# Two small GpSimd copies behind each scatter and gather of the experts

## The chip, the cores and the metric

The kernel runs on one NeuronCore of one Trainium2 chip. The metric is the device time of one execution in microseconds (us). Before the change it is 939.87 us, the median of 3 runs (939.29 to 940.05).

Engines are called as the profile calls them: PE is TensorE (matrix products, transposes), DVE is VectorE, ACT is ScalarE, POOL is GpSimd, SP is SyncE, which here only starts DMAs. "L941" is line 941 of the kernel before.

## The reference, cut to what matters

The first half is attention over 8 batches and 8 heads, 576 positions, head size 64: scores, a threshold at the row's maximum minus `tau`, softmax over what stays, times `v`. Its output is laid out as 4608 rows of 512 numbers. The second half is a mixture of 8 experts in which a row's expert follows from a hash of its token id:

```python
expert_idx = token_ids * np.int64(2654435761) % np.int64(E)
out = np.zeros((N, D), dtype=np.float32)
for e in range(E):
    mask = expert_idx == e
    xe = x[mask]
    h = np.maximum(xe @ w1[e], 0.0)
    out[mask] = h @ w2[e]
```

`w1` is 8 x 512 x 1024, `w2` is 8 x 1024 x 512, all in fp32. The change lies in the second half alone.

## The kernel before, in words

**Attention (to about 475 us).** The loop over 32 pairs of heads keeps PE, DVE and ACT in step. POOL does small work there: one threshold of 128x2 per tile (`thr`, L253), a scaling of the keys (`k_sb`, L215), and, between these, 36 indirect DMAs that write token numbers to slots in HBM (L542) and later 20 gathers for the first expert (L119). The slots come back as `stok` and `stok_odd`, 128 partitions x 8 experts x 19 int32, 152 numbers in each partition. L807 takes the smaller of the two into `stok`; after that nobody reads `stok_odd`. From `stok` come `gidx_x` (rows to gather) and `qidx` (where to scatter).

**Experts (from about 500 us).** The experts run in an order by size; the ones here are numbered in that order, 0 to 7. For expert e, layer 1 makes h = relu(w1 x) and layer 2 makes w2 h. Each layer is a two by two block product made with seven block products and sums of blocks (`seven`, L926). PE runs the seven products of a group one after the other (L941); layer 1 has two groups (g = 0, 1) of 7 x 8 matmuls, layer 2 one group of 7 x 16. PSUM has four tiles for them (`sc` and `bank`, two each), so a product may start when the product four before it has been read. DVE reads them (L861: `u`, `h`, `oT`), ACT copies the first of each group (L951, `p`) and applies the relu to finished blocks of h (L948). The sums of blocks of w1, w2, x and h that the next products need are DVE instructions too (L858 and some of L861), both of whose inputs lie in SBUF; the readers of products have one input in PSUM.

**Rows in.** `fetch(e)` (L1045) issues five gathers of 128 rows of 512 fp32 on POOL (L119) into the five `xg` buffers. DVE transposes each in 32x32 squares into `xq` (L1056), 16 DMAs of SP move `xq` into `xT` (L1064), and DVE makes the sums of x from it. `fetch(e + 2)` is called in layer 2 of expert e, at step 2; the transpositions of `xg` for expert e + 1 run in layer 1 of e and at the start of layer 2. For e = 1 a copy of one element (`mark`, L1049) stands ahead of every gather and waits for a block of h.

**Rows out.** `put_squares(e, i)` (L1024) transposes half of expert e's output into `o_q[i]` on DVE (L1028) and then issues 8 to 10 scatters of 128 pieces of 128 fp32 each on POOL (L1036). The first half is called in layer 2 of e at step 3, the second in layer 1 of e + 1. There are 17 scatters for expert 0, 18 for 1 to 4, 19 for 5 and 6. Expert 7 is put out in another way (`put_out`, four scatters, and `last_tile`, one). In program order, POOL's work is thus: the gathers of `fetch(e + 2)`, the scatters of expert e, the gathers of `fetch(e + 3)`, and so on. In the trace a run of scatters and the gathers behind it form one burst without breaks, and then POOL is idle until the next half of an output has been transposed.

**What sets the order.** The order of each engine is the one in which the code issues (`manual_schedule`); semaphores are placed by the framework. An indirect DMA of POOL takes the next of eight DMA semaphores, and waits until the DMA eight before it has landed. A gather also waits until DVE has transposed the buffer that it overwrites. A transposition into `o_q[i]` waits for the scatters that read `o_q[i]` last time. The scatters do not wait for one another's rows (`declare_no_dep`). The weights are loaded by SP two experts ahead.

Of the kernel before, what the change touches and what calls it, by code (L numbers as in the profile page):

```python
# [20 lines left out]
def kernel(  # L21
# [12 lines left out]
    nc = tc.nc  # L34
# [3 lines left out]
    E, _, F = w1.shape  # L38
# [60 lines left out]
    stok = consts.tile([P, E, NB], I32, name="stok")  # L99
    stok_odd = consts.tile([P, E, NB], I32, name="stok_odd")  # L100
# [17 lines left out]
    def gather(src, dst, idx):  # L118
        nc.gpsimd.indirect_dma_start(  # L119
            out=dst, out_offset=None, in_=src,  # L120
            in_offset=bass.IndirectOffsetOnAxis(ap=idx, axis=0),
            bounds_check=src.shape[0] - 1, oob_is_err=False)
# [704 lines left out]
    with tc.tile_pool(name="m_x", bufs=1) as m_x, \  # L827
# [169 lines left out]
        def put_out(e, *groups):  # L997
# [14 lines left out]
            for tr, kts in zip(trs, groups):  # L1012
                for i, kt in enumerate(kts):
# [7 lines left out]
                        nc.scalar.copy(dst, src)  # L1021
                    put_rows(o_sb[0:rows], gidx[0:rows, kt:kt + 1])

        def put_squares(e, i):  # L1024

            n_half = caps[e] // 64
            s0, s1 = ((0, n_half), (n_half, -(-caps[e] // 32)))[i]
            nc.vector.transpose(  # L1028
                out=o_q[i][:, 0:s1 - s0].rearrange("p n a c -> p c n a"),
                in_=oT[:, :, 32 * s0:32 * s1].rearrange("p c (n q) -> p c n q", q=32))  # L1030
            for s in range(s0, s1):
                put_rows(o_q[i][:, s - s0].rearrange("p a c -> p (a c)"), qidx[:, e, s:s + 1],
                         rows=out_q)

        def put_rows(o_sb, idx, ordered=False, rows=out):
            inst = nc.gpsimd.indirect_dma_start(  # L1036
                out=rows[:, :], out_offset=bass.IndirectOffsetOnAxis(ap=idx, axis=0),
                in_=o_sb, in_offset=None, bounds_check=rows.shape[0] - 1, oob_is_err=False)
            inst = getattr(inst, "ins", inst)
            if ordered:  # L1040
                return
            tc.declare_no_dep(inst, group="rows", reason="every token has one slot: distinct rows")
            tc.add_to_no_dep_group("rows", inst)

        def fetch(e):  # L1045
            for k in range(KT):
                if e == 1:

                    nc.gpsimd.tensor_copy(mark[0:1, :], h_0[0:1, k, 0:1])  # L1049
                gather(x_dram, xg_bufs[k][:], gidx_x[:, e, k:k + 1])  # L1050

        def turn_x(e):


            def squares(k):
                return lambda: nc.vector.transpose(  # L1056
                    out=xq[:, :, 32 * k:32 * k + 32],
                    in_=xg_bufs[k][:].rearrange("p (d a) -> p d a", a=32))

            def move():  # L1060
                for g in range(4):
                    s0, s1 = 32 * KT * g, min(32 * KT * (g + 1), caps[e])
                    for r in range(4):
                        nc.sync.dma_start(out=xT_bufs[e % 2][32 * r:32 * r + 32, :, s0:s1],  # L1064
                                          in_=xq[32 * g:32 * g + 32, r::4, 0:s1 - s0])

            return [squares(k) for k in range(KT)] + [move]

        with tc.manual_schedule():
            run(sums_w2(0), 4)  # L1070
            fill(18)
            late_h(lambda fo: (ps_sc.tile([P, 2, 512], FP32, name="sc") if fo in (2, 4) else
                               ps_m.tile([P, 2, 512], FP32, name="bank2")))
            fetch(1)
            run(sums_h(0, 0, FH), 4)

        with tc.manual_schedule():
            for e in range(E):
# [3 lines left out]
                if e > 0:  # L1082
                    w2_work, h_work = sums_w2(e), sums_h(e, 0, 2)

                    def side1(g, step):
                        if g == 0:
                            run(w2_work)
                            if step == 0:
                                put_squares(e - 1, 1)
                        else:  # L1090
                            run(h_work)
                        if step > 2:
                            run(turns, 1 if g == 0 else 2)

                    layer1(e, side1)
                    run(sums_h(e, 2, FH), 4)
                x_work = (sums_w1(e + 1) + sums_x(e + 1)) if more else []

                def side2(step):
                    if step == 0:  # L1100
                        run(turns, len(turns))
                    else:
                        run(x_work, 2)
                    if step == 2 and e + 2 < E:
                        fetch(e + 2)
                    if step == 4 and e + 2 < E:
                        load_w1(e + 2)
                    if more and step == 3:
                        put_squares(e, 0)
                    if not more and step == 4:  # L1110
                        put_out(e, (0,))
# [85 lines left out]
```

## Time and profile before

| | |
|---|---|
| time, median of 3 runs | 939.87 us |
| the profiled execution's own time | 931.3 us |
| its span, first to last instruction | 929.7 us |
| mean granted clock of TensorE | 0.996 |
| PE busy | 909.8 us, 98% |
| DVE busy | 757.5 us, 81% |
| ACT busy | 457.3 us, 49% |
| POOL busy | 403.7 us, 43% |
| scatters of experts 0 to 6 (L1036) | 127, mean 1.09 us |
| gathers for experts 1 to 7 (L119) | 35, mean 1.04 us |

One execution is profiled; all lines of the profile are from it. A group's line has the source line, the engine, the operation, what is written and read with its shape, how often, then the busy time in us with the mean of one in ns, and then the idle time of the engine just before these instructions with what ended it. A line of the timeline has start and duration in us, engine, source line, operation, and in brackets the idle time before it and who ended it; "issue" means that the profile shows nothing that was waited for, "remote" an unknown releaser. A busy time "by stretch" has the stretch, its length, the busy time of PE with the count of its instructions, the granted clock, the share of DMA time and GB/s. A line of waits has who waited for whom, and then us in total, how often, and the longest.

Ends of matmuls are modelled in the trace; their starts are recorded.

### The profile page before, as it was taken

How to read it: one execution, taken by the hardware profiler on the slowest of the kernel's cores; microseconds unless marked ns; L12 is line 12 of the kernel's file. 1: busy time of each engine (PE TensorE's matmuls, PEld its weight loads, DVE VectorE, ACT ScalarE, POOL GpSimd, SP SyncE). 2: the span in 40 equal slices, each digit the busy share in tenths (PEclk: the TensorE clock that was granted, in tenths of full speed). 3: DMA queues.
4: the chain of work that ended last, by engine and by line, in shares of the span. 5: the costliest groups of instructions: out<-in, count | busy, mean ns of one | idle time of the engine just before them, and what ended most of it. 6: DMA issues, size and time to landing. Idle time of an engine off the chain costs nothing.

```text
span 929.7 us, 20725 instructions
## 1 busy us (share of the span) xinstructions
PE 909.8 (98%) x7495; PEld 662.0 (71%) x7495; DVE 757.5 (81%) x1654; ACT 457.3 (49%) x741; POOL 403.7 (43%) x528
## 2 busy tenths in 40 slices
PE   7999999999999999999999999999999999999996
PEld 4666666656666566665678888788887978878785
DVE  7999999999999999999955776767668676777551
ACT  6888888888888898888812010110201021020110
POOL 4232432456666623455423370724527073440702
PEclk9999999999999999999999999999999999999999
DMA  7354463554545668743101745364372536412101
GB/s 175 92 148 118 109 152 93 136 131 103 123 105 153 159 165 214 216 107 88 30 25 51 237 131 158 133 173 141 95 223 75 164 133 165 157 34 50 48 3 55
DMA packets 114775, 113.11 MB, mean 122 GB/s; under 512 B 32475, under 2 KB 89315, under 8 KB 114672
## 3 DMA queue, kind: packets, MB, share of 16 engines
q1 hardware_dynamic: 105168, 92.64, 37.0%
q0 software_dynamic: 9072, 18.91, 7.0%
q8 instruction: 61, 1.00, 0.4%
q14 instruction: 42, 0.34, 0.1%
q10 hardware_dynamic: 432, 0.21, 0.1%
HBM read 81.99 MB, written 21.44 MB: 111 GB/s over the span
## 4 chain that ended last, share of the span: by engine, by line
PE 65%; issue 21%; POOL 7%; DVE 3%; ACT 2%; DMA 1%; another core or an unknown queue 1%; POOLq 0%; SPq 0%; DVEq 0%; ACTq 0%
PE av L313 18%; PE sc L235 15%; PE tr L282 11%; PE sc L941 9%; PE bank L941 8%; POOL out_dram L1036 6%; PE sc L640 2%; PE av L282 1%; POOL xg L119 1%; ACT w L260 1%; DVE ns L246 1%; DVE w L271 1%; ACT wT_b L303 1%; ACT wT_a L303 0%
## 5 line engine op out<-in xcount | busy, mean ns | idle before, releaser
L260 ACT ACTIVATE w<-ns,nmx 128x576 f32<-128x576 f32 x288 | 220.5, 777 | 28.8 <-DVE ns L246 27.8
L271 DVE SCALAR_TENSOR_TENSOR w<-ns,thr,w 128x576 f32<-128x576 f32 x288 | 225.8, 816 | 0.0
L1036 POOL DMA_INDIRECT out_dram<-o_q,qidx x127 | 138.1, 1087 | 191.7 <-DVE o_q L1028 153.1
L246 DVE TENSOR_SCALAR_CACHE_REDUCE ns<-sc 128x576 f32<-128x576 f32 x288 | 205.6, 747 | 8.1 <-PE sc L235 7.4
L253 POOL TENSOR_SCALAR thr<-nmx,drop 128x2 f32<-128x2 f32 (+1 forms) x160 | 104.4, 653 | 187.3 <-DVE ns L246 177.6
L235 PE MATMUL sc<-k_sb,q 64*128 64x288 f32 (+1 forms) x1280 | 179.2, 423 | 1.0 <-DVE drop L704 0.7
L282 PEld LDWEIGHTS tr<-ident,w 64*128 64x128 f32 x2624 | 106.0, 138 | 95.4 <-ACT wT_b L303 32.4
L282 PE MATMUL tr<-ident,w 64*128 64x64 f32 x2624 | 139.5, 231 | 6.0 <-ACT wT_b L303 2.6
L948 ACT ACTIVATE h<-h 128x576 f32<-128x576 f32 (+1 forms) x56 | 38.7, 693 | 164.8 <-DVE h L861 126.1
L235 PEld LDWEIGHTS sc<-k_sb,q 64*128 64x128 f32 (+1 forms) x1280 | 93.0, 177 | 23.2 <-DVE ns L246 9.4
L313 PE MATMUL av<-wT_a,v 128*64 128x320 f32 (+1 forms) x704 | 100.6, 418 | 0.2
L303 ACT COPY wT_a<-tr 128x512 f32<-128x512 f32 (+1 forms) x128 | 81.7, 638 | 20.7 <-PE tr L282 20.2
L303 ACT COPY wT_b<-tr 128x512 f32<-128x512 f32 (+1 forms) x128 | 81.4, 636 | 17.1 <-PE tr L282 11.2
L313 PE MATMUL av<-wT_b,v 128*64 128x256 f32 x640 | 83.2, 389 | 0.0
L313 PEld LDWEIGHTS av<-wT_a,v 128*64 128x64 f32 x704 | 43.8, 137 | 29.3 <-DVE xm L352 0.7
L951 ACT COPY p<-bank 128x576 f32<-128x576 f32 (+2 forms) x11 | 7.0, 633 | 99.5 <-PE bank L941 72.5
L313 PEld LDWEIGHTS av<-wT_b,v 128*64 128x64 f32 x640 | 40.2, 136 | 18.8 <-issue 0.7
L542 POOL DMA_INDIRECT slot_scratch<-tok,slot_i x36 | 45.0, 1251 | 9.4 <-issue 7.6
L941 PE MATMUL bank<-h,w_sb 128*128 128x288 f32 (+3 forms) x192 | 48.1, 404 | 0.0
L941 PE MATMUL sc<-h,w_sb 128*128 128x288 f32 (+3 forms) x192 | 47.7, 401 | 0.0
L941 PEld LDWEIGHTS bank<-h,w_sb 128*128 128x128 f32 x192 | 46.6, 300 | 0.5
L941 PEld LDWEIGHTS sc<-h,w_sb 128*128 128x128 f32 x192 | 45.9, 289 | 0.6
(197 smaller groups left out, 1303.7 us busy)
## 6 DMA issues: line engine op xcount, KB each, us to landing
w_sb<-in_moe_w_dram SPq DMA_DIRECT2D x16, 2048.0 KB
q<-in_q_dram SPq DMA_DIRECT2D x62, 288.0 KB
v<-in_v_dram SPq DMA_DIRECT2D x32, 256.0 KB
x_scratch<-xm SPq DMA_DIRECT2D x32, 256.0 KB
xT<-xq SPq DMA_DIRECT2D x84, 80.0 KB
k_sb<-in_k_dram SPq DMA_DIRECT2D x31, 144.0 KB
k_sb<-in_k_dram SPq DMA_DIRECT2D x32, 112.0 KB
x_scratch<-xg SPq DMA_DIRECT2D x9, 256.0 KB
```

Source lines behind the costliest of these rows:

```text
L235: nc.tensor.matmul(sc[out_rows, i, 0:S2], lhsT=q_sb[rows, h, q0:q1], rhs=k_sb[rows, h], start=True, stop=True)
L246: nc.vector.tensor_scalar(out=ns[:].rearrange("p (i s) -> p i s", i=2), in0=sc[:, :, 0:S2], scalar1=-1.0, scalar2=None, op0=ALU.mult, op1= ...
L253: nc.gpsimd.tensor_scalar(out=thr[:, 0:j + 1], in0=stats[n][0][:, 0:j + 1], scalar1=drop[:], scalar2=None, op0=ALU.add)
L260: nc.scalar.activation(w, nss[n, j][:], AF.Exp, bias=stats[n][0][:, j:j + 1], scale=-1.0)
L271: nc.vector.scalar_tensor_tensor(out=w, in0=nss.pop((n, j))[:], scalar=stats[n][1][:, j:j + 1], in1=w, op0=ALU.is_le, op1=ALU.mult, accum_ ...
L282: nc.tensor.transpose(dst[:, r, 64 * c:64 * c + 64], src[rows, c0:c0 + P], ident[rows, rows])
L303: nc.scalar.copy(dst, tr[:, :, 0:64 * n_c].rearrange("p r (c q) -> p r c q", c=n_c))
L313: nc.tensor.matmul(av[64 * j:64 * j + 64, g, c0:c1], lhsT=v_sb[:, c, 64 * j:64 * j + 64], rhs=wT[g][:, i, c0:c1], start=(c == 0), stop=stop)
L542: nc.gpsimd.indirect_dma_start(out=slot_dram[c % 2][:, :], out_offset=bass.IndirectOffsetOnAxis(ap=slot_i[:, c:c + 1], axis=0), in_=tok[:, ...
L941: nc.tensor.matmul(ps[:, i, 0:width], lhsT=lhsT, rhs=y[:, c], start=c == 0, stop=c == n_k - 1)
L948: nc.scalar.activation(c, c, AF.Relu)
L1036: inst = nc.gpsimd.indirect_dma_start(out=rows[:, :], out_offset=bass.IndirectOffsetOnAxis(ap=idx, axis=0), in_=o_sb, in_offset=None, boun ...
```

## The change

A new function `pause` issues two copies on POOL, each of the whole of `stok` (128 x 152 int32) into `stok_odd`, whose contents are no longer used. It is called behind every scatter of `put_squares`, and behind every gather of `fetch` for experts 2 to 7. It is not called behind the gathers of expert 1 or the five scatters of expert 7.

```diff
+        def pause():
+
+            for _ in range(2):
+                nc.gpsimd.tensor_copy(stok_odd[:], stok[:])
+
         def put_squares(e, i):
 ...
             for s in range(s0, s1):
                 put_rows(o_q[i][:, s - s0].rearrange("p a c -> p (a c)"), qidx[:, e, s:s + 1],
                          rows=out_q)
+                pause()
 ...
                 gather(x_dram, xg_bufs[k][:], gidx_x[:, e, k:k + 1])
+                if e > 1:
+                    pause()
```

The second copy of a pause writes what the first has written, so it waits for the first on POOL's own semaphore, and so does each pause for the pause before. No instruction of another engine waits for a copy. The order of instructions on PE, DVE, ACT and SP stays as it was.

## The prediction

> **What bounds the kernel now.** I read the page first, then the busy time of PE by expert, then the waits of PE, then the timelines of all engines through one expert. The page:
>
> ```profile
> span 929.7 us, 20725 instructions
> PE 909.8 (98%) x7495; PEld 662.0 (71%) x7495; DVE 757.5 (81%) x1654; ACT 457.3 (49%) x741; POOL 403.7 (43%) x528
> L1036 POOL DMA_INDIRECT out_dram<-o_q,qidx x127 | 138.1, 1087 | 191.7 <-DVE o_q L1028 153.1 <-issue 36.8 <-DMA out_dram<-o_q,qidx 1.8
> ```
>
> PE is the bound. POOL, which the change lengthens, is less than half busy, and its long waits are for work (the transposed output of the next expert), not for room. So the question is what POOL's activity does to PE. PE's busy time by half expert (stretch, length, busy) shows it gapless except in four stretches:
>
> ```profile
> 555.00:583.00 28.00, 26.38 (x109) 1.00 0.60 169
> 583.00:610.70 27.70, 27.70 (x116) 1.00 0.37 126
> 664.80:692.50 27.70, 27.43 (x114) 1.00 0.59 170
> 803.30:833.00 29.70, 28.94 (x113) 1.00 0.26 94
> 861.30:891.00 29.70, 28.86 (x114) 1.00 0.13 40
> ```
>
> The gaps sum to 1.62 + 0.27 + 0.76 + 0.84 = 3.5 us. That is all that experts can gain. PE's waits after 500 us name the same time:
>
> ```profile
> PE bank L941 <- DVE h_s L858: 1.9, 2, 1.6
> PE sc L941 <- ACT p L951: 0.6, 1, 0.6
> PE bank L941 <- ACT p L951: 0.5, 1, 0.5
> ```
>
> Behind these waits lies something odd. Three products of expert 4 in the PE timeline, then what VectorE reads of them, then the last gather of the POOL burst that runs beside them:
>
> ```profile
> 713.82 2.10 PE L941 MATMUL bank<-x_s,w_sb 128*128 128x288 f32 x8
> 715.76 2.10 PE L941 MATMUL sc<-xT,w_sb 128*128 128x288 f32 x8
> 717.70 2.10 PE L941 MATMUL bank<-xT,w_s 128*128 128x288 f32 x8
> ...
> 717.20 0.76 DVE L861 TENSOR_TENSOR h<-bank,u 128x576 f32<-128x576 f32 x1 [1.45 <-PE bank L941]
> 720.07 0.76 DVE L861 TENSOR_TENSOR u<-sc,u 128x576 f32<-128x576 f32 x1 [0.23 <-PE bank L941]
> 722.97 0.76 DVE L861 TENSOR_TENSOR h<-bank,u 128x576 f32<-128x576 f32 x1 [1.48 <-remote]
> ...
> 720.82 0.99 POOL L119 DMA_INDIRECT xg<-x_scratch,gidx_x  x1 [0.30 <-issue]
> ```
>
> The products end 1.94 us apart (715.8, 717.7, 719.7); their readers start 2.9 us apart, 1.4, 2.3 and 3.2 us after them. PE's release comes late and later. Other experts show the same, always in the later part of a POOL burst: after burst ends at 558.7, 721.8, 825.9 and 883.9 the late reader starts at 560.8, 723.0, 827.6 and 885.5, and all is on time again. In experts 6 and 7 lateness begins some 12 us into the burst, in the others 20 to 30 us. It is what opens PE's gaps: at 560.8 the last product of a layer is read 6.5 us late, the sums of h behind it too, and PE stops 1.6 us.
>
> [...] a two-column threshold on POOL took 0.72 us where it ran beside two-input masks (0.29 at least), and a mask 1.31 us at most (median 0.81). [...]
>
> **The change, part by part.** It adds 127 pauses behind scatters and 6 x 5 = 30 behind gathers: 157 pauses, 314 copies of 128x152 int32, all on POOL. Nothing is removed, and the order on PE, DVE, ACT and SP is unchanged.
>
> *One copy.* Nearest rows of POOL:
>
> ```profile
> L215 POOL TENSOR_SCALAR k_sb<-k_sb,k_scale 128x576 f32<-128x576 f32 x31 | 24.0, 774 | 2.8
> L494 POOL CAST rank<-rank_i 128x36 f32<-128x36 int32 x1 | 0.2, 214 | 0.0
> L1049 POOL COPY mark<-h 1x1 f32<-1x1 f32 x5 | 1.5, 297 | 7.8 <-ACT h L664 7.8
> ```
>
> The median of L215 is 745 ns, of L1049 177. (745 - 214) / 540 columns = 0.98 ns each, so 214 + 116 x 0.98 = 328 ns[...]. I take 0.33 us, with 0.72 (the blocked threshold) as upper end.
>
> *One pause.* A DMA follows a DMA after 0.30 us, follows a copy after 0.16 (502.03 to 502.19), and a copy follows a DMA at once. A pause adds 2 x 0.33 + 0.05 + 0.16 - 0.30 = 0.57 us without lock waits. VectorE's two-input instructions of an expert (8 of 1.21, 12 of 0.76 us in 54.6) make a copy wait (8 x 1.46 + 12 x 0.58) / (2 x 54.6) = 0.17 us on average: 0.57 to 0.91; I take 0.75; upper end 2 x 0.72 - 0.09 = 1.35.
>
> *One burst.* 18 scatters and 5 gathers run 580.4 to 612.7; 23 pauses add 17 us (13 to 31): to 630. The next o_q is ready at 634.6, so 22.1 us are free and a pause could cost 0.96 before POOL falls behind. What is later: the gathered rows, 632 instead of 614, read at 651; o_q's buffers, rewritten at 643, free by then; the xT transposition and weight loads, on SP's queue, are not behind POOL. The last burst, 858.2 to 883.9 plus 19 x 0.75 = 14, ends at 898, and the next scatter is due at 913.3. The tail is untouched. Cost on the path: 0; without cover (pause over 0.96) the excess x 23 per expert, still inside the 19 us of the gathered rows for several experts.
>
> *VectorE.* About 20 two-input instructions per expert can each meet a copy (at most 0.33 us). Only the three sums of h between the layers (L858) are near PE's path. Where releases are on time they have about 3 us of cover: at 613.8 the release was 3.2 us late and PE did not stop. Cost 0; cover gone, at most 3 x 0.33 = 1 us in each of 6 bursts.
>
> *Late releases.* The late state needs many POOL DMAs close together: it starts only after 12 to 30 us at one per 1.3 us and clears within 1.2 to 2.2 us once they stop. A backlog that builds slowly and clears fast says the burst is only a little over what can be served. Scatters two or more us apart, in attention, leave releases at most 1.2 us late. With pauses DMAs come every 2.05 us, 37% fewer per time. I expect the backlog not to form and PE's gaps to close: at most -3.5 us; I take -2.9, leaving 0.6 for lock waits.
>
> *Sum.* 929.7 - 2.9 = 926.8 span. The profiled execution took 931.3 us, 1.6 around the span; timed runs have a median of 939.87, 8.6 more than the profiled one. I carry that difference unchanged: 937.0.
>
> **Rivals.**
> Releases stay late, hidden otherwise (or lateness belongs to the recorder): the trace has fewer records of semaphore updates than instructions that make them only where POOL issues indirect DMAs (954 for 1047 on VectorE), so recording is strained there, and timed runs may have no lateness to lose. Then 939.9, within +-1.5. For it: the strained records. Against: the readers truly start late.
>
> Slower, longer lateness: if the state lasts as long as POOL is active, copies included, it goes on through the 14 us by which bursts grow. It decides in experts 6 and 7, whose bursts end inside layer 1: some 5 more products at +0.9 us, the backlog not cleared before layer 2, some 4 to 6 us each; up to 1.5 in the others: +10 us, 950 (943 to 957). It decides once a copy counts like a DMA. Against: the gaps between DMAs triple.
>
> Slower, lock: half of the 1 us in 6 bursts, with late releases kept: +3 us, 943. It needs the cover gone.
>
> **How the numbers follow.** Relief 0.45 (its own range 935.8 to 938.0), nothing 0.25, longer lateness 0.22, lock 0.08. Relief is faster by more than 0.2% (1.9 us), which is about what a measurement of this kernel tells from no change. Range: from 935.0 (all gaps closed and the timed runs holding more of them) to 948: left out are half of longer lateness (0.11) and little below (0.04).
>
> **What would show it.** Right: groups of 314 copies near 0.33 us; PE without gaps in experts 1, 6, 7; readers of g = 1 products within 0.3 us of their ends; bursts ending near 630 and 898. Wrong: readers still 2.9 us apart, gaps of over 1 us in experts 6 and 7, sums of h over 1.0 us each, or copies so slow that a burst runs into the next o_q.

## The result, and the profile after

The changed kernel takes 925.74 us, the median of 4 runs (924.33 to 926.27). Beside it stands the kernel before with 939.58 (939.29, 939.87 and 940.05, and one run of 932.84). The ratio of the comparison is 0.9887, interval 0.986 to 0.9915; the bare quotient of the medians is 0.9853, just outside that interval. So the change is faster by about 1.1% (8 to 13 us by the interval), where the prediction said 0.3% (937.0) and a range that ended at 935.0. The profiled execution after took 926.27 us, in line with its timed runs; that of before took 931.3, 8.6 less than the median of 939.87 that stood beside it then. A run more than 1.5% above the fastest of its kernel counts as slow here and is left out of medians and ratios; five of the 20 runs of one experiment, copies last in set 2, are such, and no others.

The page of the changed kernel, the lines that answer to those of before, and the new copies:

```profile
span 924.6 us, 21039 instructions
PE 906.9 (98%) x7495; PEld 661.6 (72%) x7495; DVE 759.9 (82%) x1654; ACT 457.3 (49%) x741; POOL 550.1 (59%) x842
L1042 POOL DMA_INDIRECT out_dram<-o_q,qidx x127 | 139.7, 1100 | 57.8 <-issue 49.2
L1027 POOL COPY stok_odd<-stok 128x152 int32<-128x152 int32 x314 | 139.9, 445 | 10.0
```

POOL works 146 us longer (403.7 before). Its idle time before scatters fell from 191.7 to 57.8 us, and of what is left 49.2 is not a wait for anyone: POOL now goes from one burst into the next nearly without rest. That cost PE nothing. Here is PE's busy time in the stretches that answer to the half experts shown of before, shifted by what the traces are apart at each place (stretch, length, busy):

```profile
555.60:583.60 28.00, 28.00 (x117) 1.00 0.65 190
583.60:611.30 27.70, 27.70 (x116) 1.00 0.27 91
663.40:691.10 27.70, 27.70 (x116) 1.00 0.57 171
800.10:829.80 29.70, 29.70 (x120) 1.00 0.36 120
856.60:886.30 29.70, 29.70 (x119) 1.00 0.08 27
```

Length and busy time are equal in each: all gaps are closed, and the list of PE's waits after 500 us is empty. Here are the same three products of expert 4 as shown of before, then VectorE's transposition and its readings of them, then POOL's DMAs, from the timeline of all engines:

```profile
711.93 2.10 PE L941 MATMUL bank<-x_s,w_sb 128*128 128x288 f32 x8
713.87 2.10 PE L941 MATMUL sc<-xT,w_sb 128*128 128x288 f32 x8
715.81 2.10 PE L941 MATMUL bank<-xT,w_s 128*128 128x288 f32 x8
...
714.07 0.76 DVE L861 TENSOR_TENSOR h<-bank,u 128x576 f32<-128x576 f32 x1 [0.52 <-PE bank L941]
715.41 1.30 DVE L1064 STREAM_TRANSPOSE xq<-xg 128x512 f32<-128x512 f32 x2
716.63 0.72 DVE L861 TENSOR_TENSOR u<-sc,u 128x576 f32<-128x576 f32 x1
717.95 0.76 DVE L861 TENSOR_TENSOR h<-bank,u 128x576 f32<-128x576 f32 x1
...
712.12 0.98 POOL L1042 DMA_INDIRECT out_dram<-o_q,qidx  x1 [0.15 <-issue]
714.52 0.98 POOL L1042 DMA_INDIRECT out_dram<-o_q,qidx  x1 [0.43 <-issue]
716.62 0.97 POOL L1042 DMA_INDIRECT out_dram<-o_q,qidx  x1 [0.43 <-issue]
```

The products end at 714.03, 715.97 and 717.91. The first and the third are read 0.04 us later, where before they were read 1.4 and 3.2 us late. The second is read at 716.63, as soon as VectorE is done with the transposition that stands before it; before, it was read 2.3 us late. The DMAs start 2.1 to 2.4 us apart.

### The profile page after: what moved, and what is told of

Read it like the earlier page. It is cut to its first block, busy times and chain, and to the rows that moved or that the text cites. A ratio compares the mean times of both kernels' runs of the same rounds, so it can differ in the third digit from the quotient of the medians.

```text
span 924.6 us, 21039 instructions
## 1 busy us (share of the span) xinstructions
PE 906.9 (98%) x7495; PEld 661.6 (72%) x7495; DVE 759.9 (82%) x1654; ACT 457.3 (49%) x741; POOL 550.1 (59%) x842
## 3 DMA queue, kind: packets, MB, share of 16 engines
q0 software_dynamic: 9072, 18.91, 6.6%
## 4 chain that ended last, share of the span: by engine, by line
PE 83%; POOL 6%; issue 4%; DVE 3%; ACT 2%; DMA 1%; SPq 0%; POOLq 0%; DVEq 0%; ACTq 0%
PE bank L941 18%; PE av L313 18%; PE sc L941 18%; PE sc L235 14%; PE tr L282 11%; POOL out_dram L1042 4%; PE sc L640 3%; POOL stok_odd L1027 2%; PE av L282 1%; DVE ns L246 1%; DVE w L271 1%; ACT w L260 1%; DMA k_sb<-in_k_dram 1%; ACT wT_b L303 1%; PE bank L658 0%
## 5 line engine op out<-in xcount | busy, mean ns | idle before, releaser
L1042 POOL DMA_INDIRECT out_dram<-o_q,qidx x127 | 139.7, 1100 | 57.8 <-issue 49.2
L1027 POOL COPY stok_odd<-stok 128x152 int32<-128x152 int32 x314 | 139.9, 445 | 10.0
L119 POOL DMA_INDIRECT xg<-x_scratch,gidx_x x35 | 41.8, 1193 | 19.2 <-issue 9.3
L951 ACT COPY p<-sc 128x576 f32<-128x576 f32 (+2 forms) x11 | 7.0, 637 | 84.7 <-PE sc L941 79.8
```

The costliest lines, as they stand in the source:

```text
L1027: nc.gpsimd.tensor_copy(stok_odd[:], stok[:])
L1042: inst = nc.gpsimd.indirect_dma_start(out=rows[:, :], out_offset=bass.IndirectOffsetOnAxis(ap=idx, axis=0), in_=o_sb, in_offset=None, boun ...
```

## The experiments

The fifteen runs were made in four sets, each with its own runs of the kernel before beside it, and the sets fell on four different chips. That turned out to matter more than most edits: on the chip of the first set nothing is late in any kernel that was traced. Each set was made on one chip and within a few minutes, so what is called a matter of the chip below could also be one of the time. A number for the state of things, worked out from each trace by counting: from the end of PE's product number 5,701 of 7,495 (at about 490 us, in line 640, before the experts' bursts) to the end of the last one. Without stalls it is 426.0 us. The traces come from one execution each, whose time stands beside the median where the two are far apart. In several traces, with late releases and without, up to 1.2 us of the number is one wait of PE between 523 and 533 us for a sum of x (`x_s`), at the start of the first burst or before it. "Period" is the mean distance of the starts of POOL's DMAs within a burst.

| kernel, set | median, us | before beside it | ratio (interval) | period, us | 5,701 to last, us |
|---|---|---|---|---|---|
| before, first comparison (profiled: 931.3) | 939.58 | | | 1.37 to 1.59 | 431.3 |
| after, first comparison | 925.74 | 939.58 | 0.9887 (0.986 to 0.9915) | 2.45 | 426.1 |
| after, set 1 | 918.25 | 919.06 | 0.9996 (0.9987 to 1.0004) | 2.44 | 426.6 |
| scatters only, set 1 | 919.34 | 919.06 | 1.0002 (0.9995 to 1.0008) | | 427.0 |
| gathers only, set 1 | 918.09 | 919.06 | 0.9992 (0.9984 to 1.0001) | | 426.4 |
| copies last, set 1 | 918.45 | 919.06 | 0.9998 (0.999 to 1.0006) | 1.37 to 1.49 | 426.0 |
| before, set 2 (profiled: 939.01) | 935.85 | 937.84 | 0.9983 (0.9955 to 1.0011) | 1.34 to 1.45 | 439.4 |
| after, set 2 | 925.82 | 937.84 | 0.9871 (0.9823 to 0.9919) | 2.46 | 426.5 |
| copies last, set 2 (profiled: 934.84; all 20 runs: 944.75) | 943.03 | 937.84 | 1.0065 (1.004 to 1.0089) | 1.34 to 1.50 | 435.9 |
| one copy, set 2 | 926.95 | 937.84 | 0.9882 (0.9833 to 0.993) | 1.68 to 1.79 | 426.1 |
| scatters only, set 3 | 925.63 | 931.95 | 0.9942 (0.9913 to 0.9971) | | 426.6 |
| gathers only, set 3 (profiled: 926.11) | 930.33 | 931.95 | 0.9985 (0.997 to 1.0) | 1.36 to 1.68 | 427.4 |
| one element, set 3 | 925.16 | 931.95 | 0.994 (0.992 to 0.996) | 1.52 to 1.70 | 426.1 |
| three copies, set 3 | 987.01 | 931.95 | 1.0612 (1.0585 to 1.0639) | 2.81 | 485.0 |
| four behind every second, set 4 | 924.85 | 937.97 | 0.9863 (0.9824 to 0.9903) | 2.47 | 426.1 |
| 24 behind every twelfth, set 4 | 929.37 | 937.97 | 0.9898 (0.9855 to 0.994) | 1.29 to 1.61 in a dozen | 429.2 |
| no rows moved, set 4 | 935.34 | 937.97 | 0.9978 (0.996 to 0.9995) | 1.34 to 1.56 | 435.6 |

### Set 1: the change and its parts, on a chip where nothing is late

The changed kernel once more, unaltered:

> The changed kernel once more, unaltered, beside the runs of the next three experiments. Spacing theory (indirect DMAs of GpSimd that follow each other within 1.3 us make PE's releases late, and PE stalls; the timed runs of the kernel before hold about 8 us more of it than its profiled execution did): 924 to 927 us, ratio to the kernel before about 0.987. Rival (the difference between the two kernels is one of the placement of a run, and the kernel before can be fast by itself): the runs of the kernel before spread between 932 and 940, the ratio is nearer to 0.99, and the changed kernel spreads too.

The pause behind the scatters alone:

```diff
@@ def fetch(e):
-                if e > 1:
-                    pause()
```

> The pause stands behind the 127 scatters alone; the 30 gathers follow each other without one. Spacing theory: the scatters are four fifths of each burst, the five gathers at its end last 6.5 us, less than the 12 to 30 us after which releases came late: 925 to 928 us, nearly the whole gain. If the gathers (which read and write other memory than the scatters) were the source: 935 to 940.

The pause behind the gathers alone:

```diff
@@ def put_squares(e, i):
-                pause()
```

> The pause stands behind the 30 gathers alone; the 18 scatters of each burst follow each other as in the kernel before. Spacing theory: the scatters' 23 us are enough for the releases to become late, only the last part of five bursts is relieved: 934 to 939 us. If the gathers were the source: 925 to 928.

The same copies, all behind a burst's last DMA:

```diff
-        def pause():
+        def pause(n):
 
-            for _ in range(2):
+            for _ in range(2 * n):
                 nc.gpsimd.tensor_copy(stok_odd[:], stok[:])
@@ def put_squares(e, i):
-                pause()
+            if i == 1 and e + 3 >= E:
+                pause(-(-caps[e] // 32))
@@ def fetch(e):
-                if e > 1:
-                    pause()
+            if e > 1:
+                pause(KT + (-(-caps[e - 3] // 32) if e > 2 else 0))
```

> As many copies as in the changed kernel, but all of a burst's copies (46, 36 or 38 of them) stand behind its last DMA, so that the DMAs follow each other as closely as in the kernel before. The first five gathers, of the third expert, have their ten copies behind them. Spacing theory: as late as the kernel before, 937 to 942 us, ratio 0.997 to 1.003. Rival (the copies themselves, a busy GpSimd or later gathers bring the gain, not the distance between DMAs): 924 to 928, ratio 0.987.

All four medians lie between 918.09 and 919.34, and 49 runs of the kernel before between 917.63 and 919.89. None of my numbers for the spacing theory came, and the ratio of the two kernels that the first comparison had put at 0.9887 is 0.9996 here. In the timeline of the gathers-only kernel, whose scatters are as dense as those of before, expert 4 looks like this:

```profile
702.15 2.10 PE L941 MATMUL sc<-x_s,w_s 128*128 128x288 f32 x8
702.35 0.76 DVE L861 TENSOR_TENSOR u<-bank,p 128x576 f32<-128x576 f32 x1 [0.20 <-PE bank L941]
702.52 0.97 POOL L1041 DMA_INDIRECT out_dram<-o_q,qidx  x1 [0.30 <-issue]
703.80 0.97 POOL L1041 DMA_INDIRECT out_dram<-o_q,qidx  x1 [0.30 <-issue]
704.09 2.10 PE L941 MATMUL bank<-x_s,w_sb 128*128 128x288 f32 x8
704.29 0.76 DVE L861 TENSOR_TENSOR u<-sc,u 128x576 f32<-128x576 f32 x1 [0.52 <-PE sc L941]
```

Scatters start 1.28 us apart, some 20 us into the burst, and still the product that ends at 704.25 is read at 704.29. So density alone does not make a release late; on this chip it did not. (The kernel before has no trace of its own in this set; gathers only and copies last, whose scatters are as dense, stand for it.) What this set does show cleanly is the cost side: 157 pauses on POOL cost nothing measurable where they bring nothing (0.9996, interval 0.9987 to 1.0004).

A second difference runs through the traces. The records of semaphore updates are most numerous here: 1,047 to 1,049 of VectorE's (the prediction counted 1,047 instructions that make them), and 3,554 to 3,601 of those that mark the ends of the software DMAs, which is 15.9 to 16.1 for each of 224 DMAs. In the first comparison the kernel before had 954 and 1,880 of them (8.4 for each DMA), the changed one 1,002 and 3,271 (14.6); the first DMA left 16 in either trace. Every trace with late releases has lost records. But records are also lost where nothing is late: from 550 to 900 us, at 16 for each DMA, the kernel before lacks 65% of the records of its DMAs, the kernel with a single element for a copy (set 3) 32% and the changed one 8%, and in these two no release is late there. So lost records alone do not tell that releases are late.

### Set 2: a chip where releases are late

The kernel before, with a second profile of its own:

> The kernel before, unaltered, with a profile of its own. In the last four experiments the kernel before took 919.06 us beside 918.25 for the changed one, where the first comparison had 939.58 beside 925.74. Theory A (late releases are a condition of the chip or of the recording on which the first comparison was made; where it is absent the pause is worth nothing): if this execution shows PE's releases at the ends of its products, no waits of PE in the experts and no semaphore records lost (1049 of VectorE), its time is about 918 to 919 and equals that of the changed kernel; if it shows releases 2.9 us apart and some 950 records of VectorE, its time is 930 to 940. Theory B (the kernel before itself has two kinds of executions on any chip): times of both kinds appear within this one call.

> The changed kernel unaltered, as the reference for the other three on the same chip. Theory A: 918 and level with the kernel before where no records are lost; 924 to 927, some 1.3% under the kernel before, where they are. Theory B: 918 to 926 with the kernel before now and then 14 us above it.

> All copies of a burst behind its last DMA, as in the earlier experiment of this kind, where it took 918.45. If records are lost on this chip: spacing theory 937 to 942 (as the kernel before); copies-themselves theory 924 to 928. If none are lost: 918 to 919 once more, which tells nothing between the two.

One copy in place of two:

```diff
-            for _ in range(2):
+            for _ in range(1):
                 nc.gpsimd.tensor_copy(stok_odd[:], stok[:])
```

> One copy behind each DMA in place of two: period of the DMAs about 1.6 us in place of 2.1. If records are lost on this chip: spacing theory between the two kernels, 928 to 934; if one copy already gives the backlog time to clear, 924 to 927. If none are lost: 918 to 919.

Theory A holds as far as it goes: this chip shows late releases in the kernel before and loses records (956 of VectorE's), and its 31 runs lie between 932.94 and 943.31. Times of 918 never appear (Theory B falls). The changed kernel is at 925.82, and copies last, which keeps the DMAs close together, is at 943.03: the same copies, 17 us apart, by where they stand. Releases are late in its trace and PE waits for them (the changed kernel has one wait of 0.2 us there):

```profile
PE bank L941 <- DVE h_s L858: 3.0, 3, 1.4
PE sc L941 <- DVE h_s L858: 1.3, 1, 1.3
```

So the copies themselves, and a GpSimd kept busy, bring nothing; the distance they make does. One copy is enough (926.95). That copies last is even slower than the kernel before (1.0065) I did not expect from either theory, and why is not shown. Its copies make the next burst start some 5 to 7 us later in the layers of experts 4 to 6 (696.6 for 691.5, 752.7 for 745.9, 809.3 for 802.2), so that late releases fall on other products; but its one trace is of the fastest of its 20 runs and holds less stalling (435.9) than that of the kernel before (439.4).

The second profile of the kernel before took 939.01 us, like an ordinary run. Its waits of PE after 500 us, to set beside the 3.4 us (3.0 in the three lines shown) of the first:

```profile
PE bank L941 <- DVE h_s L858: 3.1, 2, 1.9
PE sc L941 <- DVE h L861: 2.9, 2, 2.7
PE bank L941 <- DVE h L861: 2.9, 2, 2.6
PE bank L941 <- DVE x_s L858: 0.8, 1, 0.8
```

The last of them, for `x_s`, is the wait near the start of the first burst named above. And what opens one of the others, in expert 7, from the timeline of all engines:

```profile
879.40 2.18 PE L941 MATMUL sc<-xT,w_sb 128*128 128x300 f32 x8
881.42 2.18 PE L941 MATMUL bank<-xT,w_sb 128*128 128x300 f32 x8
883.85 2.26 PE L941 MATMUL sc<-x_s,w_s 128*128 128x300 f32 x8 [0.24 <-DVE h L861]
...
885.05 0.98 POOL L1036 DMA_INDIRECT out_dram<-o_q,qidx  x1 [0.31 <-issue]
886.34 0.98 POOL L1036 DMA_INDIRECT out_dram<-o_q,qidx  x1 [0.30 <-issue]
887.89 0.78 DVE L861 TENSOR_TENSOR h<-bank,u 128x600 f32<-128x600 f32 x1 [4.19 <-remote]
888.73 3.81 PE L941 MATMUL bank<-x_s,w_s 128*128 128x300 f32 x8 [2.62 <-DVE h L861]
```

The product in `bank` ends at 883.60 and is read at 887.89, 4.3 us late and 0.6 us after POOL's last scatter of this burst ends; PE waits 2.62 us for the bank. And then it is slower for a while:

```profile
861.00:896.00 35.00, 32.14 (x120) 0.95 0.11 36
```

The number after the products in brackets is the granted clock: 0.95 over these 35 us. In the record of the clock it is one stretch of 3.4 us at half speed, which begins at 889.3, just after PE goes on. If half speed costs half of these 3.4 us, the stop costs its own length and then some 1.7 us more (an estimate). That it follows from the stop is not shown: another stop of the same length in this trace, 2.66 us long and over at 828.8, has no such stretch behind it.

### Set 3: which DMAs, how much distance, and how much is too much

Scatters only and gathers only again (the edits of set 1):

> The pause behind the 127 scatters alone, as in the earlier experiment of this kind (919.34 on a chip on which no kernel showed late releases). If this chip shows them: spacing theory 925 to 930, since the five gathers at a burst's end last 6.5 us, less than the 12 us after which releases came late at the earliest; if the gathers matter alone, 935 to 940. If this chip doesn't show them: 918 to 920, level with the kernel before.

> The pause behind the 30 gathers alone (918.09 in the earlier experiment of this kind). If this chip shows late releases: spacing theory 932 to 940, as the 18 scatters of a burst still follow each other at 1.29 us for 23 us; if the gathers were the source, 925 to 928. If it doesn't: 918 to 920.

One element in place of the 128x152:

```diff
-            for _ in range(2):
-                nc.gpsimd.tensor_copy(stok_odd[:], stok[:])
+            nc.gpsimd.tensor_copy(stok_odd[0:1, 0:1, 0:1], stok[0:1, 0:1, 0:1])
```

> One copy of a single element in place of the two of 128x152: an instruction stands between the DMAs, but they start every 1.3 to 1.5 us in place of 2.1 (a one-element copy took 0.18 us at the median, and the step from a copy to a DMA is 0.16 where that from DMA to DMA is 0.30). If this chip shows late releases: distance is what counts, then 932 to 940; an instruction of any length between two DMAs is enough, then 925 to 928. If it doesn't: 918 to 920.

Three copies in place of two:

```diff
-            for _ in range(2):
+            for _ in range(3):
                 nc.gpsimd.tensor_copy(stok_odd[:], stok[:])
```

> Three copies behind each DMA: a period of some 2.5 us, 23 of them 58 us, over the 54.6 us of an expert, so that GpSimd falls behind by some 3 us with each expert and the last scatters end about 25 us later than with two copies (906 us there). Cover theory of the prediction (a pause that costs more than the free time of GpSimd is paid): 932 to 950 on any chip, with PE or the last output tiles waiting. Rival (there is more cover than I counted, the gathered rows are early enough and the end does not depend on the scatters): within 2 us of the changed kernel, 925 to 928 or 918 to 920.

This chip shows late releases too, less of them (before 931.95). Scatters alone take what the changed kernel reached elsewhere (925.63; the changed kernel itself was not run in this set), gathers alone take 1.6 us of the kernel before's 931.95 (ratio 0.9985, with an interval that ends at 1.0), and their trace is of the fastest of 20 runs. In it releases are late in four of the seven bursts, so dense scatters are enough. That fits the expectation, in which the scatters count because they are 18 in a row.

The single element was a miss: I expected no gain, and it is level with the rest (925.16). The timeline of POOL in that kernel shows why the test was not the one I meant:

```profile
595.16 0.98 POOL L1041 DMA_INDIRECT out_dram<-o_q,qidx  x1 [0.16 <-issue]
596.14 0.18 POOL L1026 COPY stok_odd<-stok 1x1 int32<-1x1 int32 x1
596.48 0.98 POOL L1041 DMA_INDIRECT out_dram<-o_q,qidx  x1 [0.16 <-issue]
...
602.67 0.98 POOL L1041 DMA_INDIRECT out_dram<-o_q,qidx  x1 [0.16 <-issue]
603.65 0.81 POOL L1026 COPY stok_odd<-stok 1x1 int32<-1x1 int32 x1
604.61 0.98 POOL L1041 DMA_INDIRECT out_dram<-o_q,qidx  x1 [0.16 <-issue]
```

Left alone, the copy takes 0.18 us and the DMAs are 1.32 apart. But others take up to 0.81, so the mean copy is 0.37 and the mean period 1.52 to 1.70. (What stands beside such a copy shows in the traces of the first comparison. Of the five one-element copies `mark` of the kernel before, four took 0.18 us and the fifth, at 503.22 beside VectorE's sums of h, 0.78. Of the 314 copies of the changed kernel, the 216 that no VectorE sum of two SBUF inputs overlaps took 0.31 to 0.33 us, the 98 that one overlaps 0.73 on average and 1.28 at most.) So either a period of 1.5 us is enough, or an instruction between two DMAs. Set 4 bears on it.

Three copies show what POOL's spare time, the cover of the prediction, is worth. PE's waits of that kernel after 500 us, then VectorE's longest:

```profile
PE bank L941 <- DVE u L861: 26.3, 3, 10.6
PE sc L941 <- DVE u L861: 18.9, 2, 11.7
```

```profile
DVE o_q L1033 <- DMA out_dram<-o_q,qidx: 54.0, 6, 14.6
```

VectorE stops 54 us, six times, at the transposition that rewrites `o_q`: the scatters that read that buffer are not done. PE waits behind it for sums that VectorE owes it, and the kernel is at 987.01. The mean clock granted is 0.97 there. So the time that POOL has to spare ends between two copies (mean distance 2.45 us, no wait) and three (2.81), and what gives way first is the buffer, not the gathered rows.

### Set 4: rate or adjacency, rows or issue

What was still open before this set: the prediction had taken the stalls of one execution for all that is there; and it was undecided whether the mean rate counts or DMAs with nothing between, and whether the moved rows or their issue.

Four copies behind every second DMA, then 24 behind every twelfth:

```diff
+        behind = []
+
         def pause():
 
-            for _ in range(2):
+            behind.append(1)
+            for _ in range(2 * 2 if len(behind) % 2 == 0 else 0):
                 nc.gpsimd.tensor_copy(stok_odd[:], stok[:])
```

> The same copies, but four behind every second DMA in place of two behind each: half of the DMAs follow another at 1.29 us, and the mean period stays near 2.1 us. If the chip shows late releases in the kernel before (930 to 940 there): a matter of the mean rate, 925 to 927 as the changed kernel; a matter of DMAs with nothing between, about half of the gain, 928 to 933. If the chip shows none: 918 to 920.

> The same copies, 24 behind every twelfth DMA: up to twelve DMAs follow each other at 1.29 us, then some 10 us without one. If the chip shows late releases in the kernel before: a backlog that needs 12 to 30 us of dense DMAs and clears in 1 to 2 us gives 925 to 929; a matter of DMAs with nothing between, within 2 us of the kernel before. If the chip shows none: 918 to 920.

The kernel before, with a limit on the rows that the experts' scatters may write, which leaves out nearly all of the output:

```diff
-                in_=o_sb, in_offset=None, bounds_check=rows.shape[0] - 1, oob_is_err=False)
+                in_=o_sb, in_offset=None,
+                bounds_check=3 if rows is out_q else rows.shape[0] - 1, oob_is_err=False)
```

> The kernel before, with the limit of the scatters' row numbers at 3: nearly all rows of the result that the experts' scatters would write are left out, and GpSimd issues the same 127 scatters at the same distances. If the moved rows (their packets, or what signals their end) make the releases late: 925 to 927 on a chip where the kernel before has 930 to 940. If the issue by GpSimd does: as the kernel before, 930 to 940. If the chip shows none: 918 to 920.

*Rate.* With pairs some 1.3 us apart nothing is late in the experts, and the time is that of the changed kernel, 924.85. From the timeline of POOL:

```profile
602.74 1.08 POOL L1045 DMA_INDIRECT out_dram<-o_q,qidx  x1 [0.43 <-issue]
604.12 0.97 POOL L1045 DMA_INDIRECT out_dram<-o_q,qidx  x1 [0.30 <-issue]
605.09 1.45 POOL L1030 COPY stok_odd<-stok 128x152 int32<-128x152 int32 x4
607.03 0.98 POOL L1045 DMA_INDIRECT out_dram<-o_q,qidx  x1 [0.49 <-DVE u L861]
```

So two DMAs may follow each other with nothing between. With dozens, which have the same copies and nearly the same rate over a whole burst, most of the gain is there (929.37), but releases are late within and behind the dozens (18 times by more than 0.15 us between 500 and 900 us, none with pairs), and of the 3.2 us of stalls 1.9 come with them (the other 1.2 are the wait for `x_s`, at 532.5). So what counts is the rate over a stretch longer than two DMAs, and 15 us of dense DMAs are already enough for late releases. Whether a period of 1.5 us would do without an instruction between the DMAs is not shown: the pairs have 2.47 us on average.

*Issue.* With the rows left out the software DMAs move 10.77 MB in place of 18.91, in as many packets (the page of the kernel before, then of this one):

```profile
q0 software_dynamic: 9072, 18.91, 7.0%
q0 software_dynamic: 9072, 10.77, 4.8%
```

The time is still 935.34, 0.2% under the kernel before, with 30 updates of PE's semaphore more than 0.15 us behind a product's end between 500 and 900 us, where the kernel before has 29 (in the first comparison and in set 2 alike) and the changed one none. So it is not the moved data, or only the smallest part. What stays the same in that kernel is the issue by POOL (127 scatters) and the number of packets (9,072).

## Why the prediction was wrong

**The step that failed: "I carry that difference unchanged".** The profiled execution of before was 8.6 us faster than the timed median, and I took these 8.6 us for something outside the change. The timed runs of the first comparison have no trace, but an ordinary run has, and it shows more of the same late releases in that place. The second profile of the kernel before, on another chip and at 939.01 us, holds 439.4 us from product 5,701 to the last where the first, at 931.3, holds 431.3, and the part ahead of it is the same within 0.4 us (490.6 and 491.0). So 13.4 us of stalls in the experts, not 5.3; 1.0 of them is the wait for `x_s`, some 1.7 (the estimate above) the half-speed stretch behind a late release, and the rest sits at late releases. The sum ought to have been: 5.2 us that the profiled execution loses, and 8.6 that timed runs lose besides, 13.8; the quotient of the medians says 939.58 - 925.74 = 13.84, the ratio 8 to 13. That the sum comes so close proves little, since the profiled and the timed runs of the changed kernel agree within 0.5 us; the second profile is the evidence. An 8.6 us difference between a profiled execution and three timed ones that agree within 0.8 was a fact to be explained, and lateness, already in view in the trace, was the first candidate. My range did name it ("the timed runs holding more of them") and gave it 1.4 us beside the 0.6 of closed gaps, without a reason; so it could not reach what followed.

**A smaller error in the same step: "That is all that experts can gain".** The 3.5 us were PE's idle time. From product 5,701 to the last, before against after, 431.30 - 426.07 = 5.23 us went away in the very traces the sum was made on; PE's idle time is 3.49 of it, and its busy time the other 1.74 (427.81 and 426.07). Matrix product by matrix product, nearly all of that sits at the edges of the late reads. A matmul's modelled end lies 0.16 us behind the place where the next would have started, so that each of six stops is read that much too short, and the first matmul behind a stop takes 0.49 to 0.52 us in place of 0.41. Idle time alone was a lower bound and I called it a ceiling, and then took 2.9 of it.

**Right: the mechanism, as far as the runs reach.** Releases come late where POOL's DMAs are dense, some ten us into a burst (12 in the kernel without rows, 16.5 in experts 6 and 7 of the kernel before), they are on time again soon after it (the late readers that the prediction names start 1.2 to 2.1 us behind a burst's end), and distance removes this. Copies last (943.03) against the changed kernel (925.82), with the same copies, and pairs (924.85) against dozens (929.37) show it; that a backlog builds behind it is a picture that fits, and what would be in the backlog is not shown. The mean over a whole burst gives no limit: bursts with means of 1.34 to 1.68 us have late releases (1.59 in the kernel before, 1.68 in gathers only), since a break or a paced end raises the mean, and bursts of 1.52 to 1.70 in the one-element kernel have none. The densest twelve DMAs of a burst tell them apart better: 1.31 to 1.39 us on average in the bursts of the kernel before, 1.45 to 1.57 in the one-element kernel. "PE without gaps" came exactly, and "readers within 0.3 us of product ends" did where VectorE was free.

The prediction read attention as support, and it was half of a warning. Beside the DMAs there, 1.6 us apart and more, PE's releases come up to 1.05 us late too, 34 times by more than 0.15 us in the kernel before and 32 times in the changed one, and not once in the changed kernel of set 1. So dense DMAs are not the only ones beside which releases are late, and 1.5 us between DMAs is enough in the experts alone. The "12 us" into the bursts of experts 6 and 7 is not in the lines of the first profile either: the first late reader there comes 16.5 us into the burst (816.7 and 874.7); in the kernel without rows it comes after 12.

**Right: cost on the path 0, lock cost 0**, and shown apart from any gain on the chip of set 1 (0.9996). "Lock" is the prediction's word for what its thresholds and masks show: a POOL instruction and a two-input one of VectorE can each take longer where they meet (in the kernel before a threshold 0.72 us beside a mask, against 0.29 at least; a mask 1.31 beside the scaling of the keys, against a median of 0.81).

**Off in size, without effect: the pause.** A copy has a median of 0.317 us, as predicted (0.33), and a mean of 0.445, since the 98 that meet a VectorE sum took 0.73 on average. But I had a DMA follow a copy after 0.16 us; that holds behind a copy that was held up (0.15), and behind an undisturbed pair it is 0.43 or more. A pause adds 2.45 - 1.42 = 1.03 us, not 0.75, above the 0.96 that I named as the point where POOL falls behind. It did fall behind: from 530 to 906 us it never rests over 4 us, the gathers behind the second burst end at 641 in place of 632, the last burst at 906 in place of 898. The first of these gathered rows are read at 649.8, so nothing was late. Where cover really ends, with three copies, o_q's buffer stops VectorE first, which the prediction had dismissed as "free by then"; the price of a third copy is 61 us, not an excess that the gathered rows' 19 us would soak up.

**The rivals.** "Nothing" is what the chip of set 1 shows, though for another reason than I gave: there is no lateness to lose, in the timed runs or in the traces. "Longer lateness" (950) fell: in copies last the late updates stop within 2.7 us of the end of a burst's last DMA although copies follow for 15 us and more, so copies do not count like DMAs. "Lock" fell: where there is no lateness to set it off, the pauses cost nothing (0.9996).

**What stays open.** Why three chips show it and one doesn't (or three stretches of time and one), and whether the chip itself is slow to pass signals on or the recording is. Every trace with late releases has lost records, though not the other way round, and no run shows what the one has to do with the other. Every execution here has a span, so each was recorded; there is none without to set beside it. Nor did the change touch attention, where some 6 to 8 us more are lost (product 5,701 ends at 489.6 to 491.6 us in the first comparison and sets 2 to 4, at 482.9 to 484.2 in set 1, with and without the pause): that is where the changed kernel's 925.7 in the first comparison and 918.3 in set 1 part, with the experts alike. Releases are late in attention where this time is lost; that they cost it was not tested.

## What to carry to other kernels

When a profiled execution and the timed runs differ by more than the runs among themselves, work out what the timed runs contain that the profiled one lacks before summing anything; it may be the very term that the change acts on. When signals of an engine arrive late and steps apart while another engine issues a dozen or more indirect DMAs back to back, try that engine's issue rate: here a little distance (1.5 us per DMA and more, with a copy between) removed the lateness in the experts, though not that in attention, and one copy (926.95), a single element (925.16) or pairs with a pause (924.85) do as well as two copies each (925.82), as long as the issuing engine has the time. Time a change that moves a per cent on more than one chip: the distance is worth 1.1 to 1.4% in the first comparison and in sets 2 and 4, 0.6% in set 3 and nothing in set 1; no version here beat the changed kernel by more than the intervals.

## What the runs showed of the hardware that I had not expected

- The same kernel took 919.06 us on one chip (49 runs within 2.3 us) and 931.95, 937.84 and 937.97 on three others (9.7 to 10.4 us spread each), at a granted clock of 0.99 and more. The traces put the difference in attention (product 5,701 ends at 489.6 to 491.6 us on the three, at 482.9 to 484.2 on the one) and in the experts (435.9 to 439.4 us from there to the last product with dense DMAs in set 2, 426.0 and 426.4 in set 1), where releases are late on those three; whether chip or time decides was not tested.
- In the traces of the three chips and of the first comparison, PE's completions reach other engines in steps of 2.9 us, up to 4.3 us late (in the second profile of the kernel before), once GpSimd's indirect DMAs have followed each other for some ten us (12 in the kernel without rows; the densest twelve of a burst at 1.31 to 1.39 us in the kernel before); with one element copied between them (1.45 us and more) they are on time in the experts. Without most of the scattered rows (10.77 MB moved for 18.91) there were 30 late updates for 29. Whether the chip or its recording is what is late stays open.
- A GpSimd copy of a single element took 0.18 us alone, 0.78 beside VectorE's sums of h in the kernel before, and up to 0.81 in the one-element kernel. A DMA starts 0.15 us after a copy that was held up or a one-element copy, and 0.43 or more after two whole copies that were not held up.
- While the experts run, stretches at half clock stand only beside stops of PE of 2.6 us or more, in all 17 traces: one of 3.4 us in the second profile of the kernel before (stop of 2.62 us), one of 3.4 us in the kernel without rows (2.65), and five of 6.8 to 13.7 us with three copies (5.6 to 11.7). One stop of 2.66 us had none.
